# An explicit order for the first loads of a packed attention with a gated FFN: one k or q transfer behind each weight piece

## The chip, the core and the metric

The kernel runs on one core of one Trainium2 chip. The metric is the device time of one execution in microseconds (us), lower is better. The engines are named as the profile names them: PE is TensorE (matmuls), DVE is VectorE, ACT is ScalarE, POOL is GpSimd, SP is SyncE, which issues the DMA transfers.

## The reference

Attention over 8 batches, 8 heads, 576 rows of 64, by way of 32 packed rows per head, and then a gated FFN over the 4608 rows of 512.

```python
def sm_attn(qq, kk, vv):
    s = scale * np.matmul(qq, kk.transpose(0, 1, 3, 2))
    s = s - np.max(s, axis=-1, keepdims=True)
    a = np.exp(s)
    a = a / (np.sum(a, axis=-1, keepdims=True) + 1e-09)
    return np.matmul(a, vv)
p_packed = sm_attn(p, k, v)                 # 32 rows look at 576
out = sm_attn(q, p_packed, p_packed)        # 576 rows look at 32
x = out.transpose(0, 2, 1, 3).reshape(B * S, H * D)
y = (x @ w_a * (x @ w_b)) @ w_out           # 4608x512, 512x1536 twice, 1536x512
```

The weights are float64, everything else is float32.

## The kernel before

The weights arrive as pairs of 32-bit words in 36 **pieces** of 512 KB: 24 of `w_a` and `w_b` (six chunks of four) and then 12 of `w_out`. A piece is loaded by `load_w` or `load_wout` into one of the twelve buffers of the pool `wop` (`NFT` is 12). Three steps make float32 of it: A (`high_word`, on ACT, line 203), B (`low_word`, on ACT, line 211, or on DVE or POOL, line 208) and C (`both_words`, on DVE, line 214), which frees the piece's buffer. A piece of `w_out` also has D (`split_wout`): C writes it to the one buffer `wo_f` (so the rows call it), and a cast on ACT (line 239) and a subtraction on POOL (line 91) split it into two parts, which stay in a buffer of the same pool; the next C waits until POOL has let go of `wo_f`.

Each batch has two halves of heads, e = 0 and e = 1 ("even" and "odd"). `stage1` lets the packed rows look at k: scores (line 276), maximum and its negative (`nmx`, lines 282 and 283), exponential (ACT, line 294), transposes (lines 315 to 318), and the product with v (line 325, forty small matmuls in the trace), whose result is scaled into `pp` (line 331). `stage2` lets q look at the packed result. k and q come in four transfers of 32x36x32 for each half (`load`, line 116), are turned into `xT` by DVE (line 124), and v comes in two transfers of 128x4x128 and two small ones (`load_v`, lines 171 and 175). p of a batch comes in four small ones (`load_p`, line 185).

The FFN uses the attention's result in an absorbed form: `g_tiles` (line 395) multiplies weights by the packed values, `mm1` (line 416) multiplies that by the attention weights in two halves, one for `w_a` and one for `w_b`. ACT copies the first half into `asb` (line 428), DVE multiplies the second into it (line 431), ACT casts it to `h_hi` (line 435) and POOL subtracts for `h_lo`. The copy of line 428 frees the PSUM banks of its half. Matmuls of line 442 (`mm2_part`) multiply by `w_out`. Batches 0 and 1 are done this way; the later ones go through another loop, which the change doesn't touch.

The order on each engine is written by hand, in tables of step names that `emit` reads: `FIRST` for the first loads, `START` for the stretch up to batch 0's FFN, `PLAN_0` for what stands between the mm1 halves and the f loop of batch 0 (slots divided by `|`). `S1` begins stage 1 of the odd heads, `r1` goes on with it, `Lk2`, `Lq0`, `Lv1`, `Lp2` load, `A` to `D` convert. SP takes its instructions in order. A load step issues its transfers at once, and `load_pieces` issues up to two pieces after every C and D, as long as a buffer of the pool is free:

```python
    def load_pieces(n):

        for _ in range(n):
            if unloaded and len(raws) + len(wo_hi) + len(wo_f32) < NFT:
                c, r = unloaded.pop(0)
                if c < NC:
                    load_w(c, r)
```

Each DMA that SP issues waits for the completion of the one issued eight before it.

Of the kernel before, what the change touches and what calls it, by code (L numbers as in the profile page):

```python
# [19 lines left out]
def tile_packed_attn_gated_ffn(  # L20
# [20 lines left out]
    nc = tc.nc  # L41
    B, H, S, D = q.shape
    J = p.shape[2]
    DM, DF = w_a.shape
    DO = out.shape[1]
    P = 128
    R, E = 4, 2
    NFT = DF // P
    NC = NFT // 2
    HS = S // 2  # L50
    TL = 32
    TX = S // TL
    XH = TX // 2
    TR = HS - 2 * P
# [48 lines left out]


    nats, xTs = {}, {}

    def load(src, key, b, i):


        t = ld.tile([P, R, XH, TL], F32, name=f"nat{i}")  # L110
        rows = src[b, R * i:R * i + R].rearrange("h s d -> (h s) d")
        rows = rows.rearrange("(y l u) d -> u l y d" if key == "k" else "(y u l) d -> u l y d", u=2, l=TL)
        for u in range(2):
            for w in range(2):
                g = 64 * u + 32 * w
                nc.sync.dma_start(
                    out=t[g:g + TL].rearrange("l h x d -> l (h x) d"), in_=rows[u][:, :, TL * w:TL * w + TL])
        nats[key, b, i] = t

    def turn(key, b, i):  # L120
# [43 lines left out]
    def load_v(b, e):  # L164


        t = ld.tile([P, R, NT, D], F32, name="vt") if b or e == 0 else scratch.tile([P, R, NT, D], F32, name="vt1")
        vv = v[b].rearrange("(r e) s d -> e s r d", e=E)[e]
        n = 2 if b else 4
        for i in range(4 // n):  # L170
            nc.sync.dma_start(
                out=t[:, :, n * i:n * i + n, :].rearrange("p r u d -> p r (u d)"),
                in_=vv[n * P * i:n * P * i + n * P].rearrange("(p u) r d -> p r u d", u=n).rearrange("p r u d -> p r (u d)"))
        for u in range(2):
            nc.sync.dma_start(
                out=t[TR * u:TR * u + TR, :, 4, :],
                in_=vv[4 * P:S].rearrange("(p u) r d -> u p r d", u=2)[u])
        vts[b, e] = t

    def load_p(b, queue=None):  # L180
        if b:
            t = sm.tile([P, H, TL], F32, name="p_nat", bufs=1)
            halves = p[b].rearrange("h j (g d) -> g j h d", g=2)
            for g in range(4):
                nc.sync.dma_start(out=t[J * g:J * g + J], in_=halves[g % 2])
        else:
            t = sm.tile([P, 2, 2, D], F32, name="p_nat", bufs=1)
            rows = p[b].rearrange("h j d -> (h j) d").rearrange("(p c) d -> p c d", c=2)
            x = scratch.tile([P, 2, D], F32, name="p_in")
            queue.dma_start(out=x.rearrange("p c d -> p (c d)"), in_=rows.rearrange("p c d -> p (c d)"))  # L190
            nc.vector.tensor_copy(out=t, in_=x.unsqueeze(2).broadcast_to([P, 2, 2, D]))
        p_nat[b] = t
# [25 lines left out]
    raws = {}  # L218

    def load_w(c, n):  # L220

        w, rr = (w_a, w_b)[n // 2], n % 2
        raw = wop.tile([P, 2, 2 * P, 2], U32, name="raw", tag="w")
        nc.sync.dma_start(
            out=raw.rearrange("p r f t -> p r (f t)"),
            in_=w.bitcast(U32)[2 * P * rr:2 * P * rr + 2 * P, 4 * P * c:4 * P * c + 4 * P].rearrange("(r p) f -> p r f", p=P))
        raws[c, n] = raw

    def load_wout(f):
        raw = wop.tile([P, DO, 2], U32, name="raw", tag="w")  # L230
        nc.sync.dma_start(
            out=raw, in_=w_out.bitcast(U32)[P * f:P * f + P, :].rearrange("p (n t) -> p n t", t=2))
        raws[NC, f] = raw

    wo_hi, wo_lo, wo_f32 = [], [], []
# [246 lines left out]
    def emit(b, plan, tasks={}):  # L482

        for name in plan.split():
            if name in tasks:
                next(tasks[name], None)
                continue
            if name == "Z":
                warm_first()
                continue  # L490
            if name in "Ww":
                warm(9 if name == "W" else 1)
                continue
            if name in "ABCD":
                convert(name)
                continue
            what, e = name[:-1], int(name[-1])
            n = b + (e // 2 if b or what[0] == "L" else 0)
            if n >= B:
                continue  # L500
            if what == "S":
                if e == 0:
                    st[b] = [stage1(b, 0), stage1(b, 1), stage2(b, 0), stage2(b, 1)]
                next(st[b][e])
            elif what == "s":
                next(st[b][2 + e], None)
            elif what == "r":
                next(st[b][e], None)
            elif what == "T":
                turn_p(n)  # L510
            elif what == "P":
                turned(ppT[:, b % 2:b % 2 + 2], pp.pop(b), b % 2)
            elif what in ("k", "q"):
                turn(what, n, e % 2) if b else turn_first(what, e)
            elif what == "Lk":
                load(k, "k", n, e % 2)
            elif what == "Lq":
                load(q, "q", n, e % 2)
            elif what == "Lv":
                load_v(n, e % 2)  # L520
            elif what == "Lp":
                load_p(n)

    st = {}

# [4 lines left out]
        x = bank_pair()[:, 0, :]  # L530
        nc.tensor.matmul(out=x[:, 0:2 * P], lhsT=zero[:, 0:P], rhs=zero, start=True, stop=True)

    FIRST = ("k0 P0 K1 k2 q0 q1 v0 q2 v1 w1 w1 w1 w1 w1 w1 w1 w1 w1 w1 w1")
    START = ("Z Z Z Z T0 k0 k1 k2 k4 k3 q0 S0 S1 r0 r1 q1 q2 r1 r0 r0 r1 q4 r0 r1 q3 P0 s0 s1 B W A s0 B A A B s0 A s0 C B s1 C s1 s0 B C s1 A s1 B C Lp2 A A B s0 g s1 s0 g w s1 g C B B B C A Lk2 A C A B C A A B B Lk3 C C")
    WAYS = ("000000021020002100012012011200010010")
    TURN = ("1101110010")
    SUBS = ("0000")
# [1 line left out]
    PLAN = (" |  |  | S0 | r0 | r0 |  | r0 |  | r0 Lv1 ; S1 | r1 | r1 q0 Lk2 | r1 | r1 | q1 Lk3 Lv2 P0 |  ; s0 | s0 s0 | s0 T2 | "  # L539
            "s0 Lp4 | s0 s1 | s1 s1 | s1 | s1 | s1 | t0 t1 t2 t3 u0 | k2 |  | k3 Lq2")  # L540
    PLAN = dict(enumerate(PLAN.split("|")))
    PLAN_0 = ("A | C C | B A B A | B C C B C | A A | C | B Lv0 | C B A T0 k0 Lp2 | A A B C Lq0 | C k1 | A B A B A C | S0 B | B A r0 | C C C B A Lq1 | | | C C B r0 r0 D A A | S1 C D | B C B B A D | r1 C | A A D | r0 T2 | | q0 B r1 C B D r1 C | | A D B | C Lv1 A r1 A B D | Lk2 B C B q1 D Lk3 A A P0 | C s0 s0 D C Lp4 A B | s1 s0 | Lv2 | D | s0 s1 s0 | k2 s0 s1 C k3 | s1 | | Lq2 D s0 s1 s1 Lq3 s1")
    PLAN_0 = dict(enumerate(PLAN_0.split("|")))

    pieces = [(c, n) for c in range(NC) for n in range(4)] + [(NC, f) for f in range(NFT)]
    unloaded, to_do = list(pieces), {x: list(pieces) for x in "ABC"}

    def load_pieces(n):

        for _ in range(n):  # L550
            if unloaded and len(raws) + len(wo_hi) + len(wo_f32) < NFT:
                c, r = unloaded.pop(0)
                if c < NC:
                    load_w(c, r)
                else:
                    load_wout(r)

    def convert(x):

        if x == "D":  # L560
            if wo_f32:
                split_wout(wo_f32.pop(0))
                load_pieces(2)
            return
        if not to_do[x]:
            return
        c, n = to_do[x].pop(0)
        if (c, n) not in raws:
            load_pieces(1)
        raw = raws[c, n]  # L570
        if x == "A":
            high_word(raw)
        elif x == "B":
            low_word(raw, int(WAYS[pieces.index((c, n))]))
        else:
            assert len(to_do["A"]) <= len(to_do[x]) and len(to_do["B"]) <= len(to_do[x])
            if c < NC:
                i, rr = divmod(n, 2)
                both_words(w_ab[:, c, 2 * rr:2 * rr + 2, 2 * P * i:2 * P * i + 2 * P], raw)
            else:  # L580
                t = sm.tile([P, DO], F32, name="wo_f32", bufs=1)
                both_words(t, raw)
                wo_f32.append(t)
            del raws[c, n]
            load_pieces(2)

    def warm(n):

# [20 lines left out]
    nc.vector.memset(zero, 0.0)  # L609
    for name in FIRST.split():  # L610
        what, i = name[0].lower(), int(name[1])
        queue = nc.sync if what == name[0] else nc.scalar
        if what == "p":
            load_p(0, queue)
        elif what == "v":
            load_v(0, i)
        elif what == "w":
            load_pieces(i)
        else:
            load_first(k if what == "k" else q, what, i, queue)  # L620
    tasks = {"g": next_g(0)}
    emit(0, START, tasks)
    drain(tasks["g"])
    early.__exit__(None, None, None)
# [52 lines left out]
    for b in range(NB):  # L677
        plan = dict(PLAN if b else PLAN_0)
        slot, tasks, late_steps = [0], {"g": next_g(b + 1)} if b == 0 else {}, [""]
# [280 lines left out]
    i, c0 = tiles[-1]  # L960
# [35 lines left out]
```

## Time and profile before

| | |
|---|---|
| median of 3 runs | 710.82 us (709.99 to 711.28) |
| profiled execution, its own time | 712.88 us |
| its span in the profile | 711.1 us |
| PE busy | 699.6 us, 98% of the span |
| DVE, POOL, ACT busy | 449.5, 410.7, 364.7 us |
| DMA packets under 512 bytes | 145744 of 180371 |
| chain that ended last | PE 89%, DMA 7% |

The span is what the profiler saw between the first and the last instruction; the time of an execution contains it and some 2 us around it. The shares of the chain say which engine the end waited for, followed back from the last instruction.

### The profile page before, as it was taken

How to read it: one execution, taken by the hardware profiler on the slowest of the kernel's cores; microseconds unless marked ns; L12 is line 12 of the kernel's file. 1: busy time of each engine (PE TensorE's matmuls, PEld its weight loads, DVE VectorE, ACT ScalarE, POOL GpSimd, SP SyncE). 2: the span in 40 equal slices, each digit the busy share in tenths (PEclk: the TensorE clock that was granted, in tenths of full speed). 3: DMA queues.
4: the chain of work that ended last, by engine and by line, in shares of the span. 5: the costliest groups of instructions: out<-in, count | busy, mean ns of one | idle time of the engine just before them, and what ended most of it. 6: DMA issues, size and time to landing. Idle time of an engine off the chain costs nothing.

```text
span 711.1 us, 14173 instructions
## 1 busy us (share of the span) xinstructions
PE 699.6 (98%) x5542; PEld 574.8 (81%) x5542; DVE 449.5 (63%) x825; ACT 364.7 (51%) x731; POOL 410.7 (58%) x320
## 2 busy tenths in 40 slices
PE   8999989999999999999999999999999999999998
PEld 6487867888778887887888788788788888888886
DVE  4988645367355669665875678765785667754342
ACT  5988734454344455644563456554555445544510
POOL 0556633337334787745874579566775577856520
PEclk9999999999999999999999999999999999999999
DMA  9999962668344745556444573456246323133002
GB/s 311 378 212 321 244 127 62 184 152 289 90 96 141 217 93 144 136 138 148 136 105 125 143 191 94 108 177 168 72 103 176 105 90 120 60 118 119 1 1 74
DMA packets 180371, 102.57 MB, mean 144 GB/s; under 512 B 145744, under 2 KB 161744, under 8 KB 174928
## 3 DMA queue, kind: packets, MB, share of 16 engines
q1 hardware_dynamic: 179888, 101.08, 50.8%
q8 instruction: 43, 0.70, 0.4%
q10 hardware_dynamic: 416, 0.59, 0.2%
q14 instruction: 24, 0.20, 0.1%
HBM read 85.92 MB, written 15.73 MB: 143 GB/s over the span
## 4 chain that ended last, share of the span: by engine, by line
PE 89%; DMA 7%; DVE 1%; ACT 1%; SPq 1%; issue 1%; DVEq 0%; ACTq 0%
PE x L764 37%; PE m L805 29%; PE m L416 8%; PE x L819 5%; PE m L442 4%; DMA raw<-in_moe_w_a_dram 2%; DMA vt<-in_v_dram 2%; PE s L325 2%; DMA raw<-in_moe_w_out_dram 1%; PE s L340 1%; PE s L276 1%; PE x L395 1%; PE s L315 1%; DMA wr<-w_kept 1%; DMA nat<-in_k_dram 1%
## 5 line engine op out<-in xcount | busy, mean ns | idle before, releaser
L764 PE MATMUL x<-wo,h_hi 128*128 128x512 f32 (+1 forms) x776 | 249.3, 391 | 0.3 <-ACT gs L825 0.3
L91 POOL TENSOR_TENSOR h_lo<-asb,h_hi 128x576 fp32r<-128x576 f32 x96 | 140.0, 1460 | 89.2 <-ACT h_hi L435 45.1
L764 PEld LDWEIGHTS x<-wo,h_hi 128*128 128x128 f32 x776 | 140.8, 188 | 22.4 <-ACT gs L825 1.3
L764 PE MATMUL x<-wo,h_lo 128*128 128x512 f32 (+1 forms) x388 | 152.0, 392 | 0.0
L91 POOL TENSOR_TENSOR G_lo<-gs,G_hi 128x640 fp32r<-128x640 f32 x72 | 112.9, 1573 | 30.9 <-ACT G_hi L840 30.6
L764 PEld LDWEIGHTS x<-wo,h_lo 128*128 128x128 f32 x388 | 72.9, 188 | 11.7
L91 POOL TENSOR_TENSOR A_lo<-gs,A_hi 128x256 fp32r<-128x256 f32 x36 | 27.2, 755 | 89.3 <-ACT A_hi L828 89.3
L887 DVE TENSOR_TENSOR d<-m,d 128x576 f32<-128x576 f32 (+1 forms) x73 | 54.1, 741 | 34.9 <-ACT d L883 34.1
L900 DVE TENSOR_TENSOR asb<-m,d 128x288 f32<-128x288 f32 x72 | 32.5, 451 | 64.1 <-ACT c L896 60.7
L896 ACT COPY c<-m 128x288 f32<-128x288 f32 x72 | 28.7, 399 | 83.2 <-PE m L805 83.2
L774 DVE TENSOR_TENSOR part<-x,part 128x512 f32<-128x512 f32 (+1 forms) x65 | 44.1, 678 | 38.7 <-PE x L764 38.7
L805 PE MATMUL m<-tx_hi,G_hi 128*128 128x288 f32 x216 | 63.8, 295 | 0.0
L805 PE MATMUL m<-tx_hi,G_lo 128*128 128x288 f32 x216 | 63.7, 295 | 0.0
L825 ACT COPY gs<-x 128x512 f32<-128x512 f32 x36 | 21.1, 587 | 83.0 <-PE x L819 81.4
L805 PE MATMUL m<-tx_lo,G_hi 128*128 128x288 f32 x216 | 63.3, 293 | 0.0
L840 ACT CAST G_hi<-gs 128x640 fp32r<-128x640 f32 x72 | 52.2, 729 | 15.1 <-POOL gs L834 14.5
L883 ACT COPY d<-m 128x576 f32<-128x576 f32 (+1 forms) x73 | 46.7, 639 | 20.1 <-PE m L805 18.5
L850 ACT CAST h_hi<-asb 128x576 fp32r<-128x576 f32 x72 | 49.0, 680 | 11.5 <-DVE asb L914 11.5
L805 PEld LDWEIGHTS m<-a_hi,G_hi 128*128 128x128 f32 x144 | 27.0, 187 | 31.8 <-issue 17.4
L834 POOL TENSOR_TENSOR gs<-gs 128x512 f32<-128x512 f32 x36 | 46.6, 1295 | 2.6 <-DVE gs L831 2.5
L805 PE MATMUL m<-a_hi,G_hi 128*128 128x288 f32 x144 | 46.6, 324 | 0.0
L913 DVE TENSOR_TENSOR m<-m,c 128x288 f32<-128x288 f32 x72 | 33.3, 463 | 17.7 <-PE m L805 16.0
(168 smaller groups left out, 1553.5 us busy)
## 6 DMA issues: line engine op xcount, KB each, us to landing
wr<-w_kept SPq DMA_DIRECT2D x36, 1024.0 KB, 5.1
nat<-in_k_dram SPq DMA_DIRECT2D x56, 144.0 KB, 5.3
nat<-in_q_dram SPq DMA_DIRECT2D x56, 144.0 KB, 5.3
vt<-in_v_dram SPq DMA_DIRECT2D x28, 256.0 KB, 3.6
out_dram<-part SPq DMA_DIRECT2D x27, 256.0 KB, 2.0
raw<-in_moe_w_a_dram SPq DMA_DIRECT2D x12, 512.0 KB, 8.4
raw<-in_moe_w_b_dram SPq DMA_DIRECT2D x12, 512.0 KB, 9.6
raw<-in_moe_w_out_dram SPq DMA_DIRECT2D x12, 512.0 KB, 6.9
```

The costliest lines, as they stand in the source:

```text
L91: return eng.tensor_tensor(out=dst, in0=src, in1=hi.bitcast(F32), op=ALU.subtract)
L416: nc.tensor.matmul(out=ps[:, half, 0:HS], lhsT=gt[:, kt, ft % 4, cols], rhs=at[:, kt, HS * half:HS * half + HS], start=(n == 0 and kt == 0 ...
L764: nc.tensor.matmul(out=o[:, cols], lhsT=ht[:, c0:c0 + P], rhs=wt[:, cols], start=(ft == fts[0] and n == 0), stop=end)
L774: nc.vector.tensor_tensor(out=parts[i][:, cols], in0=o[:, cols], in1=parts[i][:, cols], op=ALU.add)
L805: nc.tensor.matmul(out=bank[:, n % 2, 0:HS], lhsT=g, rhs=t, start=(first and i == 0), stop=(i == 2), skip_group_check=True)
L819: nc.tensor.matmul(out=gps[e][J * r:J * r + J, :], lhsT=ppT[rows, 2 * (b % 2), r, :], rhs=w[rows, r, :], start=True, stop=True)
L834: nc.gpsimd.tensor_tensor(out=gs[:, 2:4].rearrange("p a u f -> p a (u f)"), in0=gs[:, 0:2].rearrange("p a u f -> p a (u f)"), in1=s2.unsqu ...
L840: nc.scalar.copy(out=G_hi[:, n % 3], in_=gs[:, 1:6, n % 2])
L850: nc.scalar.copy(out=view(h_hi[ft]), in_=src)
L883: nc.scalar.copy(out=d[:, both], in_=X[:, both, 0:HS])
L887: nc.vector.tensor_tensor(out=d[:, both], in0=V[:, both, 0:HS], in1=d[:, both], op=ALU.add)
L913: nc.vector.tensor_tensor(out=v, in0=v, in1=c2, op=ALU.add)
```

## The change

SP's loads up to those of batch 1 and the first of batch 2 get an order of their own, the list `LOADS`. The loads of k, q, v and p no longer issue their transfers: they append them to `parcels`. `advance` goes through the list: `w` issues the next piece if a buffer of the pool is free, any other letter issues the next transfer of `parcels`, and where neither can be done it returns and is called again after the next C, D or load step. When the list is used up, transfers are issued as they come. `load_pieces` is gone.

```diff
     nats, xTs = {}, {}
+    parcels, turns_of = [], []
+
+    def advance():
+
+        while turns_of or parcels:
+            weight = turns_of and turns_of[0] == "w"
+            if weight and len(raws) + len(wo_hi) + len(wo_f32) == NFT or not weight and not parcels:
+                return
+            if turns_of:
+                turns_of.pop(0)
+            if weight:
+                c, r = unloaded.pop(0)
+                if c < NC:
+                    load_w(c, r)
+                else:
+                    load_wout(r)
+            else:
+                out, in_ = parcels.pop(0)
+                nc.sync.dma_start(out=out, in_=in_)
...
-                nc.sync.dma_start(
-                    out=t[g:g + TL].rearrange("l h x d -> l (h x) d"), in_=rows[u][:, :, TL * w:TL * w + TL])
+                parcels.append((t[g:g + TL].rearrange("l h x d -> l (h x) d"), rows[u][:, :, TL * w:TL * w + TL]))
...
-                nc.sync.dma_start(out=t[J * g:J * g + J], in_=halves[g % 2])
+                parcels.append((t[J * g:J * g + J], halves[g % 2]))
...
+    LOADS = ("w w w w w w w w w w w w w w w p p p p w k w k w k w k w k w k w k w k w v v v v w q w q w q w q w q w q w q w q "
+             "w v v v v w w w p p p p")
...
-                load_pieces(2)
+                advance()
...
-            load_pieces(2)
+            advance()
```

`load_v` appends in the same way, `emit` calls `advance` after a load step, and `FIRST` ends in one `w1` instead of eleven. `START` and `PLAN_0` are changed with it: `Lp2`, `Lk2`, `Lk3`, `Lq0`, `Lq1` and `Lv1` stand earlier, `Lp4` and `T2` later, and `S1` stands one mm1 half later, with the last step of `r0` ahead of it. What that does to the order of instructions on the engines follows at the three places that matter. (The line numbers of after are 17 higher in most of the functions; `nat` is k or q as loaded, `raw` a piece, `vt` v.)

SyncE first, behind the p of batch 1, where k of batch 1 is loaded. Before:

```order
L224 DMA raw<-in_moe_w_a_dram 128x2x512 x2
L116 DMA nat_455<-in_k_dram 32x36x32 x4
L224 DMA raw<-in_moe_w_b_dram 128x2x512 x2
L116 DMA nat_473<-in_k_dram 32x36x32 x4
L224 DMA raw<-in_moe_w_a_dram 128x2x512 x2
```

After:

```order
L241 DMA raw<-in_moe_w_b_dram 128x2x512
L124 DMA nat_393<-in_k_dram 32x36x32
L241 DMA raw<-in_moe_w_a_dram 128x2x512
L124 DMA nat_393<-in_k_dram 32x36x32
L241 DMA raw<-in_moe_w_a_dram 128x2x512
L124 DMA nat_393<-in_k_dram 32x36x32
```

The two groups of four k transfers are spread over eight pieces, so that the last k stands behind the 23rd piece where it stood behind the 20th; one more piece of `w_b` follows it.

SyncE again, at the last pieces of `w_out`, with the second half of batch 1's q (`nat_874`, after `nat_748`) and its odd v. Before:

```order
L231 DMA raw<-in_moe_w_out_dram 128x1024 x5
L116 DMA nat_874<-in_q_dram 32x36x32 x4
L231 DMA raw<-in_moe_w_out_dram 128x1024
L171 DMA vt<-in_v_dram 128x4x128 x2
L175 DMA vt<-in_v_dram 32x4x64 x2
```

After:

```order
L248 DMA raw<-in_moe_w_out_dram 128x1024
L124 DMA nat_748<-in_q_dram 32x36x32
L248 DMA raw<-in_moe_w_out_dram 128x1024
L124 DMA vt<-in_v_dram 128x4x128 x2
L124 DMA vt<-in_v_dram 32x4x64 x2
L248 DMA raw<-in_moe_w_out_dram 128x1024 x3
```

Each of the eight q transfers has a piece ahead of it, and the odd v stands ahead of the last three pieces.

VectorE from the tenth `asb` (the product of the tenth `mm1`'s halves) to the twelfth, where `S1` has its reduce. Before:

```order
L431 TENSOR_TENSOR asb<-m,asb 128x576
L282 TENSOR_REDUCE nmx<-s 128x1
L283 TENSOR_SCALAR nmx<-nmx 128x1
L214 SCALAR_TENSOR_TENSOR wo_f_1055<-raw 128x512
L431 TENSOR_TENSOR asb<-m,asb 128x576
L331 TENSOR_SCALAR pp<-s,rs 128x64 x2
L249 STREAM_TRANSPOSE pT<-p_nat 128x256
```

After:

```order
L448 TENSOR_TENSOR asb<-m,asb 128x576
L231 SCALAR_TENSOR_TENSOR wo_f_1078<-raw 128x512
L299 TENSOR_REDUCE nmx<-s 128x1
L300 TENSOR_SCALAR nmx<-nmx 128x1
L448 TENSOR_TENSOR asb<-m,asb 128x576 x2
```

The reduce and `nmx` stand behind the conversion of a `w_out` piece; `pp` has gone behind the ninth `asb`, and `pT` behind a later stage.

ScalarE at the same place. Before:

```order
L435 CAST h_hi_506<-asb 128x576
L294 ACTIVATE t_1052,rs<-s,nmx 128x576
L428 COPY asb<-m 128x576
L203 ACTIVATE raw<-raw 128x512 x2
L239 CAST wo<-wo_f_1055 128x512
L435 CAST h_hi_508<-asb 128x576
L428 COPY asb<-m 128x576
```

After:

```order
L452 CAST h_hi_505<-asb 128x576
L445 COPY asb<-m 128x576
L311 ACTIVATE t_1098,rs<-s,nmx 128x576
L220 ACTIVATE raw<-raw 128x512 x2
L256 CAST wo<-wo_f_1078 128x512
L452 CAST h_hi_507<-asb 128x576
L445 COPY asb<-m 128x576
```

The exponential of the odd heads and the copy of a mm1 half have changed places.

## Rows read from the trace of the kernel before

**Rows 1.** Page, busy time of the engines (us, share of the span, instructions).

```profile
PE 699.6 (98%) x5542; PEld 574.8 (81%) x5542; DVE 449.5 (63%) x825; ACT 364.7 (51%) x731; POOL 410.7 (58%) x320
```

**Rows 2.** Chain that ended last, 40 to 105 us: start us, us, what.

```profile
75.94 0.83 PE s L325 x40
...
86.63 5.64 DMA vt<-in_v_dram
...
92.76 4.29 PE m L442 x12
...
97.27 2.75 PE m L442 x12
```

**Rows 3.** PE's timeline, 88 to 93 us: start us, us, instruction, [idle before <-releaser].

```profile
88.53 0.39 PE L442 MATMUL m<-wo,h_lo 128*128 128x512 f32 x1
90.26 0.43 PE L325 MATMUL s<-vt,t 128*32 128x64 f32 x16 [1.34 <-DMA vt<-in_v_dram]
...
92.69 1.22 PE L442 MATMUL m<-wo,h_hi 128*128 128x512 f32 x2
```

**Rows 4.** Windows, one: stretch, busy us by engine, granted clock, DMA share, GB/s.

```profile
93.00:94.00 1.00, 1.00 (x3) 0.81 (x3) 1.00 (x4) 0.25 (x1) 0.00 (x0) 0.50 0.83 132
```

**Rows 5.** Timeline of SP's DMA issues, 35 to 85 us.

```profile
35.48 6.38 SPq L116 DMA_DIRECT2D nat<-in_k_dram  x4
...
74.99 9.36 SPq L116 DMA_DIRECT2D nat<-in_q_dram  x4
```

**Rows 6.** Windows, three others, with k or q transfers under way.

```profile
39.50:42.00 2.50, 2.50 (x27) 1.50 (x27) 2.50 (x3) 2.35 (x4) 1.62 (x2) 1.00 0.27 41
...
49.00:52.00 3.00, 3.00 (x28) 2.74 (x21) 2.12 (x4) 2.56 (x5) 0.70 (x1) 1.00 0.92 122
...
125.00:130.00 5.00, 5.00 (x69) 4.25 (x75) 1.28 (x2) 1.31 (x2) 1.42 (x1) 1.00 1.13 183
```

**Rows 7.** Timeline of ScalarE (ACT), 54 to 56 us.

```profile
54.43 0.69 ACT L203 ACTIVATE raw<-raw 128x512 f32<-128x512 f32 x1 [1.69 <-DMA raw<-in_moe_w_a_dram]
55.77 0.67 ACT L203 ACTIVATE raw<-raw 128x512 f32<-128x512 f32 x1 [0.66 <-DMA raw<-in_moe_w_a_dram]
```

**Rows 8.** Timeline of GpSimd (POOL) at 30 us.

```profile
29.92 2.33 POOL L208 TENSOR_SCALAR raw<-raw 128x512 uint32<-128x512 uint32 x1 [1.55 <-DMA raw<-in_moe_w_b_dram]
```

**Rows 9.** Timeline of VectorE (DVE), 52 to 58 us.

```profile
52.17 1.38 DVE L124 STREAM_TRANSPOSE xT<-nat 128x1152 f32<-128x1152 f32 x1 [1.05 <-DMA nat<-in_k_dram]
...
57.12 0.43 DVE L208 TENSOR_SCALAR raw<-raw 128x512 uint32<-128x512 uint32 x1 [0.79 <-DMA raw<-in_moe_w_b_dram]
```

**Rows 10.** Timeline of PE, 53 to 81 us.

```profile
53.60 0.71 PE L276 MATMUL s<-xT,pT 64*32 64x288 f32 x20 [0.28 <-DVE xT L124]
...
63.65 0.53 PE L416 MATMUL m<-a_hi,ghi 128*128 128x288 f32 x2 [0.98 <-ACT asb L428]
...
78.41 0.43 PE L416 MATMUL m<-a_hi,ghi 128*128 128x288 f32 x2
...
80.47 0.70 PE L442 MATMUL m<-wo,h_hi 128*128 128x512 f32 x2
```

**Rows 11.** Timeline of VectorE, 68 to 78 us.

```profile
68.79 0.69 DVE L214 SCALAR_TENSOR_TENSOR wo_f<-raw 128x512 uint32<-128x512 uint32 x1 [0.27 <-POOL wo L91]
...
73.96 0.74 DVE L282 TENSOR_REDUCE nmx<-s 128x1 f32<-128x576 f32 x1
74.73 0.15 DVE L283 TENSOR_SCALAR nmx<-nmx 128x1 f32<-128x1 f32 x1
75.59 1.90 DVE L214 SCALAR_TENSOR_TENSOR wo_f<-raw 128x512 uint32<-128x512 uint32 x1 [0.70 <-POOL wo L91]
77.41 0.75 DVE L431 TENSOR_TENSOR asb<-m,asb 128x576 f32<-128x576 f32 x1
```

**Rows 12.** Timeline of ScalarE, 74 to 79 us.

```profile
74.92 0.74 ACT L294 ACTIVATE t<-s,nmx 128x576 f32<-128x576 f32 x1 [0.18 <-DVE nmx L283]
...
78.77 0.63 ACT L428 COPY asb<-m 128x576 f32<-128x576 f32 x1
```

More of the change, by code (lines that the diff above doesn't have):

```diff
@@ L170, in load_v @@
         for i in range(4 // n):
-            nc.sync.dma_start(
-                out=t[:, :, n * i:n * i + n, :].rearrange("p r u d -> p r (u d)"),
-                in_=vv[n * P * i:n * P * i + n * P].rearrange("(p u) r d -> p r u d", u=n).rearrange("p r u d -> p r (u d)"))
+            parcels.append((
+                t[:, :, n * i:n * i + n, :].rearrange("p r u d -> p r (u d)"),
+                vv[n * P * i:n * P * i + n * P].rearrange("(p u) r d -> p r u d", u=n).rearrange("p r u d -> p r (u d)")))
         for u in range(2):
-            nc.sync.dma_start(
-                out=t[TR * u:TR * u + TR, :, 4, :],
-                in_=vv[4 * P:S].rearrange("(p u) r d -> u p r d", u=2)[u])
+            parcels.append((
+                t[TR * u:TR * u + TR, :, 4, :], vv[4 * P:S].rearrange("(p u) r d -> u p r d", u=2)[u]))
         vts[b, e] = t
@@ L531, in warm_first @@
         nc.tensor.matmul(out=x[:, 0:2 * P], lhsT=zero[:, 0:P], rhs=zero, start=True, stop=True)
-    FIRST = ("k0 P0 K1 k2 q0 q1 v0 q2 v1 w1 w1 w1 w1 w1 w1 w1 w1 w1 w1 w1")
-    START = ("Z Z Z Z T0 k0 k1 k2 k4 k3 q0 S0 S1 r0 r1 q1 q2 r1 r0 r0 r1 q4 r0 r1 q3 P0 s0 s1 B W A s0 B A A B s0 A s0 C B s1 C s1 s0 B C s1 A s1 B C Lp2 A A B s0 g s1 s0 g w s1 g C B B B C A Lk2 A C A B C A A B B Lk3 C C")
+    FIRST = ("k0 P0 K1 k2 q0 q1 v0 q2 v1 w1")
+    START = ("Z Z Z Z T0 k0 k1 k2 k4 k3 q0 S0 S1 r0 r1 q1 q2 r1 r0 r0 r1 q4 r0 r1 q3 P0 s0 s1 B W A s0 B A A B s0 A s0 C B s1 C Lp2 Lk2 Lk3 s1 s0 B C s1 A s1 B C A A B s0 g s1 s0 g w s1 g C B B B C A A C A B C A A B B C C")
+    LOADS = ("w w w w w w w w w w w w w w w p p p p w k w k w k w k w k w k w k w k w v v v v w q w q w q w q w q w q w q w q "
+             "w v v v v w w w p p p p")
     WAYS = ("000000021020002100012012011200010010")
@@ L541, in tile_packed_attn_gated_ffn @@
     PLAN = dict(enumerate(PLAN.split("|")))
-    PLAN_0 = ("A | C C | B A B A | B C C B C | A A | C | B Lv0 | C B A T0 k0 Lp2 | A A B C Lq0 | C k1 | A B A B A C | S0 B | B A r0 | C C C B A Lq1 | | | C C B r0 r0 D A A | S1 C D | B C B B A D | r1 C | A A D | r0 T2 | | q0 B r1 C B D r1 C | | A D B | C Lv1 A r1 A B D | Lk2 B C B q1 D Lk3 A A P0 | C s0 s0 D C Lp4 A B | s1 s0 | Lv2 | D | s0 s1 s0 | k2 s0 s1 C k3 | s1 | | Lq2 D s0 s1 s1 Lq3 s1")
+    PLAN_0 = ("A | C C | B A B A | B C C B C | A A | C | B Lv0 | C B A T0 k0 Lq0 | A A B C | C k1 Lq1 | A B A B A C | S0 B | B A r0 | C C C B A | | | C C B r0 r0 D A A | r0 Lv1 C D | S1 B C B B A D Lp2 | C | r1 A A D | | | q0 B r1 C B D r1 C | | A D B | C A r1 A B D | Lk2 B C B q1 D Lk3 A A P0 | C s0 s0 D C A B | s1 s0 T2 | Lv2 | D Lp4 | s0 s1 s0 | k2 s0 s1 C k3 | s1 | | Lq2 D s0 s1 s1 Lq3 s1")
     PLAN_0 = dict(enumerate(PLAN_0.split("|")))
@@ L546, in tile_packed_attn_gated_ffn @@
     unloaded, to_do = list(pieces), {x: list(pieces) for x in "ABC"}
[L548 to L556, printed above, removed]
     def convert(x):
@@ L567, in convert @@
         c, n = to_do[x].pop(0)
-        if (c, n) not in raws:
-            load_pieces(1)
         raw = raws[c, n]
@@ L584, in convert @@
             del raws[c, n]
-            load_pieces(2)
+            advance()
     def warm(n):
@@ L616, in tile_packed_attn_gated_ffn @@
             load_v(0, i)
+            advance()
         elif what == "w":
-            load_pieces(i)
+            turns_of.extend(LOADS.split())
+            advance()
         else:
```

## The prediction, made before the changed kernel was run

> **What bounds the kernel now.** I read the page first. TensorE (PE) is busy for 699.6 of 711.1 us [rows 1], so the kernel is bound by matmuls, and only time in which PE stands still or runs at the low clock can be won. The chain of waits, read next, shows where a DMA holds PE up for long: it goes through a load of `vt`, the values of batch 1, for 5.64 us, and right behind it twelve matmuls of line 442 take 4.29 us where the next twelve take 2.75 [rows 2]. The timeline of PE shows the place: the last matmul of that kind ends at 88.92 (88.53 + 0.39), the next one starts at 92.69, and between them stand only the forty small matmuls of stage 1 with e = 1, which wait for `vt` [rows 3]. The forty for e = 0 took 0.83 us when nothing held them up [rows 2]. The windows say why the matmuls behind the wait are slow: in 93 to 94 us the granted clock is 0.50, the lower of the two levels, 1.2 GHz, after an engine that had stood nearly idle since 88.92 [rows 4].
>
> Then the queue. SyncE (SP) issues in order, and before the odd `vt` it had to issue four q transfers at a stretch, for 9.36 us; further up four k transfers take it 6.38 us, and the next four little less [rows 5]. In 39.5 to 42 us, while SP stands in the first such group, the core moves 41 GB/s; in 49 to 52, with k transfers in front, 122 [rows 6]. So the first 90 us are bound by loads, and some of that time the DMA engines have little to do because SP can't hand out the next piece. Back to back, weight pieces come 1.34 us apart (ScalarE takes one up at 54.43, and the next, for which it also waits, at 55.77) [rows 7]: 524 kB in 1.34 us is 391 GB/s.
>
> **The change part by part.** The order of SP says that no DMA is added or dropped; each of the eight k and eight q transfers now stands behind a piece, and the odd `vt` moves from behind the twelfth piece of `w_out` to behind its ninth.
>
> *a, the odd v.* New time of its landing: after the last k (53.2, below) come one piece, the even v, eight pairs of a `w_out` piece and a q transfer, one more piece, then the odd v. A pair costs 1.34 + 0.81 = 2.15 us, eight 17.2; the rest is two pieces (2.7) and two v loads of 590 kB, at the rate of a piece 1.5 us each, together 3.0. The sum is 76, say 78 for waits on SP. PE wants it at 88.9, so it comes 11 us early, and 4 us early with the dearest k and q below. The stall goes: 92.69 − 88.92 − 0.83 = 2.94 us. The low clock goes with it, as PE has no other standstill there: 4.29 − 2.75 = 1.54. **−4.48.** If the stall stays, so do both.
>
> *b, the last k of batch 1.* Its price is the one that before does not show: a k transfer (147.5 kB in runs of 128 bytes) with a piece beside it. The nearest row is 125 to 130 us, transfers of this form (q and k of batch 2 on) mostly by themselves on full engines: 183 GB/s, 0.81 us [rows 6]. The upper bound is the 122 GB/s of 49 to 52, 1.21 us [rows 6]; the lower is zero above its bytes, 147.5 kB at 391 GB/s, 0.38 us. I take 0.81, since with a piece always queued the engines should be as full as in 125 to 130 (share 1.13), which they were not when SP stood (0.92; at equal share 122 would be 150 GB/s, 0.98 us). GpSimd waits for the eleventh piece until 29.92 [rows 8]. From there: four pieces (5.4) and the p transfers (131 kB at 183 GB/s, 0.7) give 36.0; eight pieces (10.7) and eight k (6.5) give 53.2. Now the last k is taken up at 52.17 by the transpose that waited for it, and PE, which needs the result for batch 1's first scores, then waited 0.28 [rows 9, 10]. So PE is late by 53.2 − 52.1: **+1.1** (+4.3 at 1.21 us a transfer; a gain is excluded by PE itself, at most 0.3).
>
> By the Trainium skill, "DMA: Bandwidth & Descriptors", section Bandwidth, its Measured part, an engine needs about 10.5 ns for each small packet. A k transfer is 32 × 36 runs, 72 on each of 16 engines, so 0.76 us, an estimate from that page; the sum below would be 0.4 us less. It agrees with the 183 GB/s row and not with the 122 one, and it says that putting a piece between two k transfers makes neither cheaper: the change can win only by leaving no gap.
>
> *c, what that delay is hidden behind.* For 0.98 us, until 63.65, PE stands for ScalarE's copy of a mm1 half [rows 10]. ScalarE was late there because it had waited 1.69 and 0.66 us for pieces [rows 7]; those pieces now land about 5 us earlier (the first of the two at 36.0 + 6 × 1.34 + 5 × 0.81 = 48.1, against 54.4). The exponential in between doesn't take the delay over: it waits on VectorE's reduce, ahead of which VectorE stood 0.79 us for another such piece [rows 9]. So PE comes 1.1 us later to a copy that is no longer late: **−0.98.** If ScalarE is late for another reason, this term is zero.
>
> *d, VectorE around the eleventh mm1.* The conversion of the fourth `w_out` piece now stands ahead of the reduce and its small companion (0.74 + 0.15, 0.92 with their gap). Before, these two filled most of the time until GpSimd let go of `wo_f`; then the 0.70 wait and the conversion of 1.90 us followed, and the product `asb` ran from 77.41 to 78.16, 0.25 ahead of the matmuls that start at 78.41 [rows 10, 11]. Now conversion, reduce, and then `asb`: 0.9 later on VectorE, 0.25 of it covered, **+0.65**. Bounds: 0 if the conversion takes the 0.69 us of an earlier one [rows 11], and +0.9.
>
> *e, ScalarE.* The exponential of batch 1's odd scores now stands behind the eleventh mm1's copy, no longer ahead of it, and still ahead of two `high_word`, a cast, `h_hi` and the copy of 78.77 [rows 12]. It waits for the reduce, now done at about 78.3, not at 74.9. Behind it 0.9 (itself) + 1.25 + 0.6 + 0.65 bring the copy to 81.3 to 81.9, done 0.6 later. That copy frees the PSUM banks for the first matmuls of line 442, which start at 80.47, and at 81.1 with d. **+0.85** (0 to +1.1).
>
> *At no cost.* The early `pp` and the later `pT` are small operations of VectorE; `pp` falls into the stretch in which it waits for `wo_f`, and `pT` goes, by the order, between the two transposes of stage 2, behind the last stage-1 matmuls. The scores of line 276 are moved one mm1 half, and their reduce moves back too. SP must find the buffers of k, q and `vt` free: the first q goes to the buffer that the transpose of k's first half leaves before the one of 52.17, and SP comes to it after 53.2 plus a piece and the even v. Were a buffer not free, SP would stand and every piece behind it be late; the cover is the 11 us of a.
>
> **Sum.** −4.48 + 1.1 − 0.98 + 0.65 + 0.85 = −2.86. The profiled execution took 712.88 us around a span of 711.1, so it would take 710.0; the median of the runs is 710.82, and 2.86 less is **708.0**.
>
> **The rivals.** *More gain (R1).* d and e don't happen, because VectorE's conversion is 0.7 and not 1.9 us once it starts away from GpSimd's `h_lo`; and a k is cheaper, so that b is 0.3 or so. For it speaks the 0.69; against it that the 1.90 us began right when GpSimd let go of `wo_f`, as it will again [rows 11]. −4.48 + 0.3 − 0.98 and 0 to 0.3: about 705.9.
>
> *Slower (R2).* The k transfers, mixed with pieces, take 1.2 us each. The eighth lands at 56.5, PE waits 4.3 more at its first scores: −4.48 + 4.3 − 0.98 + 1.5 = +0.3, and after so long a wait PE can fall to 0.50 there as it did at 93 to 94, another 1.5: about 712.7. It decides from 1.15 us a transfer on (last k after 56.1). For it speaks the 122 GB/s row; against it, the lower share of the engines in that row.
>
> *No change to speak of (R3).* SP stands as long as before, since it waits for the completion of the DMA eight ahead whatever the order; or the wait moves to the scores (last k at 55) and the gain of a is used up: 710 to 711. Against it speaks that the engines are idle (share 0.27) where SP stands in a group [rows 6]: one transfer between two pieces leaves them work.
>
> **How the numbers follow.** The forecast has 0.53, R1 0.20, R2 0.13, R3 0.14. The forecast's own range is 706.8 to 709.3 (d and e each between their bounds, b between 0.3 and 2). The range that leaves out at most 2 in 10 reaches from R1 to the upper end of R3, 705.6 to 711.0. A difference under 0.2% (1.4 us) can't be told from no change by a measurement of this kernel. Faster by more than that: the forecast nearly whole, R1, a little of R3, 0.69; slower: R2 and an odd part, 0.13; the rest 0.18.
>
> **What would show it.** a: no wait for `vt` near 89 us, and a granted clock of 1.00 from 88 to 96. b: VectorE's second transpose of k starts at 53.2 (52.7 to 54). c: no wait for ScalarE's copy around 63. d and e: PE's first matmul of line 442 starts 0.85 us behind the copy that frees its banks, and waits for it. SP should stand for no more than 2 us in any one issue between 35 and 55 us. The prediction fails if the transpose of k starts after 55, if the clock falls at that wait, or if a wait of the size of a appears where the loads of batch 2, now issued ahead of nothing, come too late.

## The result, and the profile after

The changed kernel is slower: median 717.65 us (715.47 to 718.68, 7 runs) against 710.82 (708.24 to 714.3, 7 runs of before on the same chip), ratio 1.0086, interval 1.0057 to 1.0114. Its profiled execution took 716.52 us, with a span of 714.7.

PE is busy as long as before to within 1 us [rows 1]; the time is standstill, and some work at the low clock. The page of after:

```profile
PE 700.6 (98%) x5542; PEld 576.1 (81%) x5542; DVE 450.4 (63%) x825; ACT 364.3 (51%) x731; POOL 410.6 (57%) x320
```

All waits of PE between 57 and 101 us, and the odd v's matmuls, in its timeline of after:

```profile
58.78 1.20 PE L293 MATMUL s<-xT,pT 64*32 64x288 f32 x20 [5.40 <-DVE xT L142]
...
85.52 0.53 PE L433 MATMUL m<-a_hi,ghi 128*128 128x288 f32 x2 [1.04 <-DVE asb L448]
...
88.42 0.72 PE L459 MATMUL m<-wo,h_hi 128*128 128x512 f32 x2 [0.49 <-ACT asb L445]
...
96.94 0.90 PE L342 MATMUL s<-vt,t 128*32 128x64 f32 x40
```

The odd v is waited for no longer (compare [rows 3]). In its place PE waits 5.4 us for the transpose of k, which before cost 0.28 [rows 10]. VectorE's timeline of after says what that transpose waits for:

```profile
57.35 1.38 DVE L142 STREAM_TRANSPOSE xT<-nat 128x1152 f32<-128x1152 f32 x1 [6.50 <-DMA nat<-in_k_dram]
```

It starts at 57.35, where before it was 52.17 [rows 9]: 5.2 us late. Windows (stretch, busy us by engine, granted clock, DMA share, GB/s), first one of before, then two of after:

```profile
38.00:51.00 13.00, 13.00 (x114) 10.99 (x113) 11.46 (x17) 10.64 (x19) 6.00 (x4) 1.00 0.91 180
```

```profile
38.00:51.00 13.00, 13.00 (x113) 10.99 (x112) 11.65 (x17) 10.65 (x20) 6.04 (x4) 1.00 1.10 260
...
60.00:62.00 2.00, 2.00 (x8) 2.00 (x9) 2.00 (x4) 0.67 (x1) 0.04 (x1) 0.50 1.17 275
```

The DMA engines have no gap (share 1.10), as was hoped, and move more than before's 180 GB/s, but 260 is less than the 312 that a pair of piece and k in 2.15 us would be. And k now has three more pieces ahead of it. Behind the standstill of 5.4 us the granted clock is 0.50, from 57.8 to 64.6 us.

One matmul after the other, by its start on PE's timeline in three executions; the second is a new execution of before that is told of below:

| matmul that starts | before, 712.88 us | before, 708.81 us | after, 716.52 us |
|---|---|---|---|
| mm1 behind batch 1's first scores | 54.25 | 54.33 | 59.92 |
| mm1, two halves on | 59.20 | 59.65 | 66.41 |
| mm1 of the 0.98 wait | 63.65 | 64.14 | 69.74 |
| last mm1 of batch 0, first half | 76.70 | 77.22 | 82.72 |
| first of line 442 (459 in after) | 80.47 | 81.00 | 88.42 |
| first of line 442 behind the odd v | 92.69 | 90.25 | 97.77 |
| twelve further on | 97.02 | 93.24 | 100.76 |

From there to the end the three run in parallel. After against the first column: +5.67 at batch 1's first scores (5.18 of it the wait for k, 0.49 the scores themselves at the low clock), +1.55 at the low clock behind them, −1.1 where before waited 0.98, +1.9 around the conversion and the exponential, −4.2 at the odd v; together, with −0.1 elsewhere, +3.7, and the spans differ by 3.6. Against the second column the last of these is missing: +7.5, and the spans differ by 7.7.

### The profile page after: what moved, and what is told of

Same layout as the page of the kernel before. It is cut to its first block, busy times and chain, and to the rows that moved or that the text cites. A ratio compares the mean times of both kernels' runs of the same rounds, so it can differ in the third digit from the quotient of the medians.

```text
span 714.7 us, 14178 instructions
## 1 busy us (share of the span) xinstructions
PE 700.6 (98%) x5542; PEld 576.1 (81%) x5542; DVE 450.4 (63%) x825; ACT 364.3 (51%) x731; POOL 410.6 (57%) x320
## 4 chain that ended last, share of the span: by engine, by line
PE 89%; DMA 6%; DVE 2%; ACT 1%; POOL 1%; issue 1%; SPq 0%; DVEq 0%
PE x L774 37%; PE m L815 29%; PE m L433 7%; PE m L459 5%; PE x L829 5%; DMA raw<-in_moe_w_a_dram 2%; PE s L342 1%; PE s L357 1%; PE s L293 1%; DMA raw<-in_moe_w_b_dram 1%; DMA vt<-in_v_dram 1%; DMA nat<-in_k_dram 1%; DMA raw<-in_moe_w_out_dram 1%; PE x L412 1%; PE s L332 1%; DVE w_ab L231 1%
## 5 line engine op out<-in xcount | busy, mean ns | idle before, releaser
L433 PE MATMUL m<-a_hi,ghi 128*128 128x288 f32 x192 | 44.2, 313 | 1.1 <-DVE asb L448 1.0
```

The costliest lines, as they stand in the source:

```text
L433: nc.tensor.matmul(out=ps[:, half, 0:HS], lhsT=gt[:, kt, ft % 4, cols], rhs=at[:, kt, HS * half:HS * half + HS], start=(n == 0 and kt == 0 ...
```

## The experiments

### The k transfers in fours (e1_k_fours)

```diff
-... w p p p p w k w k w k w k w k w k w k w k w v v v v w q ...
+... w p p p p w w w k k k k w w k k k k w w w w v v v v w q ...
```

> Theory A (alternation): a k transfer costs about 0.95 us and the piece beside it 0.3 to 0.5 us more than alone, only because small and large packets are in flight at once; in groups of four both are cheap again. Then VectorE takes up the last k at 51.5 to 53, no matmul runs at the low clock around 60, and the time falls from after's by 5.67 + 1.55 = 7 us: 709 to 711. Theory B (flat price): a k transfer costs 1.26 us wherever it stands; with eight of them and five pieces ahead of its end from 36.75 on, the last k lands at 53.5, with the holes of the queue at 55, PE waits for 1 to 3 us, and the time is 712 to 715. Theory C (the switch of the score matmuls and conversions, not the loads, makes it slower): 716 to 718 as after.

Median 713.84 us (712.74 to 715.44, 10 runs; before 709.64), ratio 1.0053 (1.0034 to 1.0072). PE's waits up to 70 us in its timeline:

```profile
53.79 0.71 PE L293 MATMUL s<-xT,pT 64*32 64x288 f32 x20 [0.16 <-DVE xT L142]
56.60 0.54 PE L433 MATMUL m<-a_hi,ghi 128*128 128x288 f32 x2 [0.29 <-DVE asb L448]
66.22 0.85 PE L433 MATMUL m<-a_hi,ghi 128*128 128x288 f32 x2 [3.34 <-ACT asb L445]
```

The wait for k is gone: the last k lands at 52.24, as theory A says (B has 53.5 to 55, C no change). This list also takes three pieces from ahead of the last k, so it does not tell alternation from place; the run after the next does. The time is only 4 us under after's, in theory B's range and not in A's 709 to 711, since a new wait stands at 66, with the granted clock at 0.50 from 65.6 to 72.4 us. ScalarE, ahead of the copy, waits 2.48 us for the first piece of `w_out`, which in after's list stands behind the even v (before had four of them ahead of it). Its timeline:

```profile
63.48 0.66 ACT L228 ACTIVATE raw<-raw 128x512 uint32<-128x512 uint32 x1 [2.48 <-DMA raw<-in_moe_w_out_dram]
```

In after that piece was as late, and the wait for k hid it. That is the first thing that the forecast didn't count.

### The reduce and the exponential ahead again (e2_r1_first)

```diff
-... | S1 B C B B A D Lp2 | C | r1 A A D | ...
+... | S1 B C B B A D Lp2 | r1 C | A A D | ...
```

> Terms d and e: with the reduce and the exponential back ahead of the conversion and the copy, the first matmul of line 459 should start 1.5 to 2 us earlier than in after (86.4 to 87 rather than 88.42). If that is worth its time, the median is 1.5 to 2 us under after's, at 715.5 to 716; the wait for k at 57 stays. Rival: the 1.9 us lost there come from late pieces and GpSimd, not from the order, and nothing changes (within 0.5 us of after).

Median 716.13 us (714.31 to 716.79, 7 runs), ratio 1.0069 (1.0041 to 1.0097). The medians lie 1.5 us apart, less than the intervals can tell; the traces tell it: both waits behind 80 us are gone, and the first matmul of line 459 starts at 86.48, 1.94 us before after's 88.42, though k came 0.5 later. At the first half of the last mm1 the two are 0.19 apart (82.53 and 82.72), so 1.75 of the 1.94 come from the order. Terms d and e are there, with 1.75 where the forecast had 1.5.

```profile
59.29 1.20 PE L293 MATMUL s<-xT,pT 64*32 64x288 f32 x20 [5.83 <-DVE xT L142]
...
86.48 0.70 PE L459 MATMUL m<-wo,h_hi 128*128 128x512 f32 x2
```

### Fours, with the last k where after has it (e4_fours_last_same)

```diff
-... w p p p p w k w k w k w k w k w k w k w k w v v v v ...
+... w p p p p w w w w k k k k w w w w k k k k w v v v v ...
```

> The order of after, but the eight k transfers in two groups of four, each behind four pieces, so that the last k stands behind the 23rd piece, as in after. Alternation as the cause: a k costs 0.8 to 0.95 us in a group and the pieces 1.34, so the last k lands at 36.8 + 8 x 1.34 + 8 x 0.95 = 55 or up to a microsecond earlier, 57.2 in after. Flat price: 57.2 as in after.

One run, 715.1 us. VectorE's timeline:

```profile
55.16 1.38 DVE L142 STREAM_TRANSPOSE xT<-nat 128x1152 f32<-128x1152 f32 x1 [4.46 <-DMA nat<-in_k_dram]
```

The last k comes 2.2 us earlier behind the same bytes, as alternation says. So of the 5.2 us by which after's k is late, 2.2 are the alternation by these two executions; the other 3.0 come with its place behind the 23rd piece, where before has it behind the 20th.

How firm the 2.2 are, the other traces tell. Take the time from the landing of batch 1's last p to that of the last k, subtract 1.34 us for each piece between, and divide by eight: a k costs 1.22 us in after and 1.30 in e2_r1_first, which loads in the same order; 0.94 here; 1.08 and 1.09 in the two traces of before; and 0.94 to 1.12 in the other runs with fours (e1, e7, e8, e10). So alternated it is dearer in every trace, by 0.1 to 0.4 us a transfer, and in no order does it cost the 0.81 of the sum.

### What in a k transfer makes the pair dear (e5_long_runs, e6_all_partitions, e9_long_and_all)

All three keep after's order and the bytes, and change only what batch 1's k transfers read and where they put it, so that batch 1's scores come from other numbers. In `load`, for k of batch 1 (`n` is 2u + w, `some` the half batch of k as rows of the length needed; one variant each, in the order of their names):

```diff
-parcels.append((t[g:g + TL].rearrange("l h x d -> l (h x) d"), rows[u][:, :, TL * w:TL * w + TL]))
+parcels.append((t[g:g + TL].rearrange("l h x d -> l (h x) d"), some.rearrange("(l c) -> l c", l=TL)))
...
+parcels.append((t[:, n], some[:, XH * (n % 2):XH * (n % 2) + XH, TL * (n // 2):TL * (n // 2) + TL]))
...
+parcels.append((t[:, n].rearrange("p x d -> p (x d)"), some[:, XH * TL * n:XH * TL * n + XH * TL]))
```

> The order of after; the eight k transfers of batch 1 have the same bytes and the same 32 partitions each, but read 4608 bytes in a row for a partition in place of 36 runs of 128 bytes (the scores of batch 1 are made from other numbers). If the short runs are what costs, a pair of piece and k costs 1.34 + 0.38 = 1.72 us, the last k lands at 36.75 + 8 x 1.72 = 50.5, and PE never waits for it. If 32 of 128 partitions as the target are what costs, the pair stays at 2.6 to 2.7 and the last k at 57.

> The order of after; each of the eight k transfers of batch 1 has as many runs of 128 bytes as before, but they go to all 128 partitions, nine to each, in place of 36 to each of 32 (the scores of batch 1 are made from other numbers). If the few partitions are what slows a mix, the pair falls to about 1.34 + 0.85 = 2.2 us and the last k lands at 54 to 55. If it is the short runs, the pair stays at 2.6 to 2.7 and the last k at 57.

> The order of after; each of the eight k transfers of batch 1 reads 1152 bytes in a row for each of 128 partitions (the scores of batch 1 are made from other numbers). Long runs alone and all partitions alone each left the pair at 2.6 us. If each was held up by the one that was left (short runs, or 32 partitions), the pair now costs 1.34 + 0.4 to 0.5 and the last k lands at 50.5 to 51.5. If alternating two kinds of transfer is what costs, whatever their form, the pair stays over 2.3 us and the last k lands at 55 or later.

One run each: 714.45, 714.48 and 707.98 us. VectorE's transpose of the last k, in this order:

```profile
56.48 1.38 DVE L146 STREAM_TRANSPOSE xT<-nat 128x1152 f32<-128x1152 f32 x1 [5.66 <-DMA nat<-in_k_dram]
```

```profile
56.38 1.38 DVE L147 STREAM_TRANSPOSE xT<-nat 128x1152 f32<-128x1152 f32 x1 [5.59 <-DMA nat<-in_k_dram]
```

```profile
51.22 1.38 DVE L147 STREAM_TRANSPOSE xT<-nat 128x1152 f32<-128x1152 f32 x1 [0.34 <-DMA nat<-in_k_dram]
```

And the window that showed 260 GB/s in after:

```profile
38.00:51.00 13.00, 13.00 (x113) 11.00 (x112) 11.83 (x17) 11.15 (x21) 6.45 (x4) 1.00 1.03 266
```

```profile
38.00:51.00 13.00, 13.00 (x114) 10.99 (x113) 11.83 (x17) 11.26 (x21) 6.45 (x5) 1.00 1.08 286
```

```profile
38.00:51.00 13.00, 13.00 (x114) 11.00 (x113) 11.84 (x17) 11.25 (x21) 6.52 (x4) 1.00 1.04 367
```

In neither of the first two does k come early: taking away the short runs alone, or the 32 partitions alone, is not enough. The third shows why: either one keeps the pair dear; without both it costs 1.8 us (by the landings in the trace the second and the eighth of these pieces lie 10.76 us apart; in after 16.49, or 2.75 a pair). Over all eight pairs, from the last p to the last k, a pair takes 2.56 us in after, 2.38 and 2.41 in the first two, and 1.73 in the third, which is 1.34 for the piece and 0.39 for the k. So an alternating order as such costs next to nothing; it is this form of k that does.

The trace's records of single packets, on all 16 engines, show where the time goes (mean duration, in brackets the median):

```
before, 14 to 29 us, pieces alone:        2048 bytes  88 ns (87)
before, 38 to 53 us, k in fours:          2048 bytes 117 ns (84)    128 bytes 13 ns (13)
after, 38 to 57 us:                       2048 bytes 115 ns (84)    128 bytes 13 ns (13)
e4_fours_last_same, 37 to 55 us:          2048 bytes 101 ns (84)    128 bytes 14 ns (13)
e5_long_runs, 38 to 57 us:                2048 bytes 127 ns (124)  4608 bytes 274 ns (265)
e6_all_partitions, 38 to 57 us:           2048 bytes 103 ns (84)    128 bytes 13 ns (13)
e9_long_and_all, 38 to 51 us:             2048 bytes  89 ns (84)   1152 bytes 56 ns (51)
```

A packet of 128 bytes takes 13 to 14 ns whoever is beside it, so a k of 72 packets for each engine is 0.95 us of engine time; the rest of the price is paid by the pieces, whose packets take longer in the mean. The median hardly moves except in e5_long_runs, so elsewhere it is a part of the packets that takes much longer. Before's fours lengthen them too (117 ns); the difference is how many pieces have a k beside them. What the packets of 2048 bytes take above 88 ns is, for each engine, 3.1 us in after (117 packets) and 1.3 in e4_fours_last_same (96 packets): an estimate from these means, and most of the 2.2 us between the two.

By the Trainium skill, "SBUF — State Buffer", section Door 1, a transfer to 32 partitions reaches only half of the 16 ports through which DMA writes. That agrees in kind with e5_long_runs, not in size: half of the 436 GB/s given there would make such a k 0.68 us, an estimate, and a pair 2.0, where the landings of e5_long_runs give 2.4 to 2.5.

### Before, once more (before_again)

> The kernel before once more, for a second trace: its profiled execution took 712.88 us, while the runs of it lie from 707.4 to 715 with a median near 710. If this one is nearer to 709, the difference shows what varies: the wait for the odd v (2.9) and the matmuls at the low clock behind it (1.5) by the sum of the forecast, so that a typical execution would have less of both to win; or something else.

708.81 us, span 707.0: 4 us under the profiled execution that the forecast worked from. Its timeline of PE at the odd v, and a window:

```profile
89.05 0.39 PE L442 MATMUL m<-wo,h_lo 128*128 128x512 f32 x1
89.37 0.95 PE L325 MATMUL s<-vt,t 128*32 128x64 f32 x40
90.25 0.73 PE L442 MATMUL m<-wo,h_hi 128*128 128x512 f32 x2
```

```profile
88.00:96.00 8.00, 8.00 (x73) 6.11 (x71) 4.29 (x7) 4.98 (x10) 3.76 (x3) 1.00 0.66 106
```

No wait for v and no low clock. The loads of this execution land within 0.7 us of the other's up to 70 us, and most of them 0.5 to 1.7 us earlier from there to the piece ahead of the odd v; the last part of v lands at 89.96, in the other one at 92.28, and PE comes to it just past 89. So this stall is one that some executions have, and the change could win it only there.

How many, the clock of the runs lets one estimate. Of the 55 runs of before that were taken beside e1, e7 and e8, 31 have a mean granted clock of 0.999 or 1.000, and a median of 708.95 us (at most 710.27); 24 have 0.998 or less, and 711.34 (at least 710.22). The second trace is of the first kind, the first trace (0.997) of the second. That is 2.4 us in 24 of 55 runs, or 1.0 in the mean; that it is the odd v in all 24, one trace can't show.

### The order that follows, and what the odd v is worth in it (e7_fours_v_early, e8_fours_v_last, e10_q_behind_pieces)

The first has k in fours at before's places, before's four pieces of `w_out` ahead of the even v, the odd v ahead of the second q, and `r1 C` of e2_r1_first (and, for the odd v to come first, the step `Lq1` behind `Lv1`). The second puts the odd v back to the end; the third puts each q behind a piece and the odd v behind them.

```diff
+... w w w w v v v v w w q q q q w w w w w v v v v q q q q w p p p p      (e7_fours_v_early)
+... w w w w v v v v w w q q q q w w w w w q q q q w v v v v p p p p      (e8_fours_v_last)
+... w w w w v v v v w q w q w q w q w q w q w q w q v v v v p p p p      (e10_q_behind_pieces)
```

> The k transfers in fours where they stood in before, four pieces of w_out ahead of the even v as in before, the odd v ahead of the second group of q, and the reduce and the exponential ahead of the conversion and the copy. By the terms as measured in after: no late k, no d and e, the wait for the odd v gone (4.3 in the profiled execution): 3 to 4.5 us under before. If before's typical execution waits less for the odd v than the profiled one, 1 to 3. If a q that comes later or a late piece takes the place of the wait: same as before.

> The version with k in fours and the odd v ahead of the second group of q, but with the odd v at its old place again, behind the second group of q and the twelfth piece of w_out. If getting the odd v earlier is worth 4.3 us, as the profiled execution of before said, this one is as slow as before (ratio 1.000). If it is worth what the second trace of before shows, nothing in most executions and up to 4 us in some, the median is within 1 us of the version with the early v (ratio 0.996 to 0.998), and the runs lie farther apart, some of them 2 to 5 us above the fastest.

> The version with k in fours, but each of the eight q transfers behind a piece of w_out, as in after, and the odd v behind the last of them. If a q beside a piece costs what a k does there, a pair takes 2.6 to 2.7 us, the last q lands at 66 + 8 x 2.65 = 87 and the odd v at 89: no or little wait of PE for it, and the time stays within 1.5 us of the version with q in fours, as nothing else waits for q. If pieces of w_out that come 1.3 us later each are waited for (by the conversions and by the last matmuls of batch 0), or the odd v comes after 90, it is 2 to 5 us slower.

| | median, us | runs | ratio to before |
|---|---|---|---|
| e7_fours_v_early | 707.67 (707.21 to 709.42) | 12 | 0.9965 (0.9951 to 0.9980) |
| e8_fours_v_last | 708.0 (707.47 to 709.54) | 12 | 0.9975 (0.9959 to 0.9991) |
| e10_q_behind_pieces | 708.65 (708.09 to 709.23) | 12 | 0.9976 (0.9960 to 0.9992) |

Before had 709.79 (708.18 to 712.98) beside the first and 709.86 (707.79 to 713.62) beside the other two. All three are a little faster than before, the first by 0.35%, its interval clear of 1. In its timeline of PE from 57 to 100 us one wait is left:

```profile
62.68 0.54 PE L433 MATMUL m<-a_hi,ghi 128*128 128x288 f32 x2 [1.03 <-ACT asb L445]
...
87.99 0.90 PE L342 MATMUL s<-vt,t 128*32 128x64 f32 x40
```

The early place of the odd v is worth 0.3 us in the medians, within the intervals: no 4.3. In e8_fours_v_last the first part of v lands at 87.85 and the last at 89.28, and the forty matmuls start at 89.55 without a wait. It had been expected that its runs lie farther apart than those of e7_fours_v_early; they don't. All 36 runs of the three have a mean clock of 0.999 or 1.000, where 24 of before's 55 have less; which of their differences from before does that is not settled (the p of batch 2, which before has between these pieces, stands at the end in all three). In the third a pair of piece and q takes 2.7 us, as a pair with k does in after, and the last q lands at 88.06, in the second at 85.15. But it costs the kernel little: the odd v lands at 88.57 to 89.78, PE's forty matmuls start at 89.10, and PE has no wait behind 64 us for the slower pieces:

```profile
89.10 1.14 PE L342 MATMUL s<-vt,t 128*32 128x64 f32 x40
```

## Why the prediction was wrong

Against the forecast's 708.0 the median is 9.7 us too long. By the two profiled executions b, the price of a k, has 4.1 of these, the low clock that came with it 2.0, and d and e 0.4; c gives back 0.1. The other 3.3 are about what a was taken too high: it counted in full a stall that many executions of before do not have.

**b failed: its price.** "I take 0.81" a transfer: the row behind it (125 to 130 us) shows such transfers by themselves. Beside pieces a k costs 1.22 us in after, and a pair 2.56 where the sum had 2.15; that is the upper bound of 1.21, and even in fours it is 0.94 or more. The row of 49 to 52 us, which gave that bound, came nearer. The chain also starts at 36.75, where the sum had 36.0. So k was taken up at 57.35, not 53.2, and PE lost 5.2 us there, not 1.1 (with the 52.17 of the row, 53.2 makes 1.0). Two of the signs by which the prediction was to fail came: a transpose of k after 55, and a falling clock at that wait. The forecast's argument for 0.81, that full engines make it cheap, was the wrong way round: they were full, and a part of the pieces' packets took longer. The sentence drawn from the Trainium skill, "DMA: Bandwidth & Descriptors", section Bandwidth, that a small packet has a price of its own, is right in kind: 13 ns here, where the Trainium skill has about 10.5, measured on transfers that GpSimd issues. That a piece between two k transfers makes neither cheaper was the prediction's own conclusion from it, and here the piece becomes dearer.

That the late k and the low clock hang on this price, e9_long_and_all shows: it is after in everything but the form of batch 1's k, has neither the wait at the first scores nor the low clock, and its one run took 707.98 us. That this is the forecast's number is chance: its k comes 2 us earlier than the forecast's, and a is worth less.

**The low clock came with the wait.** It stood with rival R2 alone, and R2's mechanism is what came true: 1.2 us a k, a long standstill at the first scores, the clock at 0.50 behind it, 1.55 us of it and 0.49 on the scores themselves. R2 had 712.7 as it counted the full gain of a, and began at 36.0.

**a failed, in its size.** Between the two profiled executions it holds: −4.2 where −4.48 was forecast, both the stall and the low clock gone. But the forecast took a term from an execution 2 us above its median and subtracted it from the median. In before_again the term is 0; by the clocks of before's runs it is about 1.0 in the mean, and in e7 against e8 it is 0.3. Its landing was wrong too: the odd v landed at 86.77, not at 76 to 78, since the q pairs were as dear as those of k. That leaves 2 us, not 11, to the 88.9 at which PE came to it in before; in after PE was late itself and came at 96.94.

**c came out in its number**: from +7.21 to +6.09 of lag over the place of the 0.98 wait, and no wait there in after. But the piece in question landed at 51.39, not 48.1, and PE came so late that it would hardly have waited in any case. In e9_long_and_all, where both k and the pieces are early, the wait is gone too. **d and e were right in place and sign**, and 1.75 us, not 1.5, by e2_r1_first, which takes them back. The conversion takes 1.90 us again, not the 0.69 that rival R1 had. **"At no cost"** held for `pp`, `pT` and p, for which no wait of PE shows, but not for the pieces: the first `w_out` piece behind the even v costs 2.5 us on ScalarE as soon as k is early enough, as e1_k_fours shows.

**SP as before** (in R3) is refuted: the DMA engines had no gap, and moved 260 GB/s against before's 180. SP stood for up to 2.3 us in one issue, a little over the 2 of the forecast's sign, where before had 4.1.

## What to carry to other kernels

A stall that a single profiled execution shows is worth its mean over executions: when that execution lies above the median, take a second trace, or size the term by the lowest runs too. Before alternating transfers to fill gaps in a queue, compare bytes per second of the mix, not the price of each kind by itself. Here the form of the small transfer was worth more than its order: 1.22 to 1.30 us alternated and 0.94 to 1.12 in fours, as short runs to 32 partitions, but 0.39 as longer runs to all 128. What must come early should have nothing put ahead of it, gap or no gap. And a wait that ends late hides the ones beneath it: before moving a load, list which other loads the same stretch will ask for once it is in time.

## What was not expected of the hardware

Transfers of k slow the pieces beside them, and either trait of their form is enough: with k to 32 partitions, or in runs of 128 bytes, or both, the core moved 260 to 286 GB/s at a share of 1.03 to 1.10, with neither 367. A busy share over 1 is thus no sign that the DMA engines are used well. Why packets of 2048 bytes take 103 to 127 ns in the mean beside k with either trait or both, and 89 ns beside k with neither, the runs don't show.
